# Rows of small blocks scattered from the tile of their sums instead of a copy

## The chip, the cores and the metric

The kernel runs on one core of a Trainium2 chip. A core has TensorE (PE in the profile; PEld is its weight loads), VectorE (DVE), ScalarE (ACT), GpSimd (POOL), SyncE (SP), and DMA engines that all of them can give work to. The metric is the device time of one execution in microseconds; the median of several runs is compared.

## The reference

Sigmoid attention over 8 batches, 12 heads, 448 tokens and head size 64 gives 3584 rows of 768. These go through a mixture of experts in which each token takes one expert of 8 (hidden size 1024), or none.

```
scores = scale * (q @ k.T) - log(S);  attn = sigmoid(scores);  x = attn @ v   # as rows, 3584 x 768
compute = (x @ w_skip) > 0                     # other rows are returned as they are
e = argmax(x @ w_gate);  gate = softmax(x @ w_gate)[e]
out = x;  out[compute] = x + gate * (relu(x @ w1[e]) @ w2[e])
```

## The kernel before

The first part of the span (to about 327 us) is the attention, step by step over pairs of heads, and the first two blocks of the mixture of experts. Each attention row is stored to the output in DRAM, and each token's gate and number are put into a list per expert.

The rest is one loop whose length is known only at run time: one pass is one block of tokens of one expert. A block takes one of four arms (`choose`, line 1515):

- FULL: 128 tokens, with the expert's weights split into a high and a low part (three matmuls for each product).
- SPLIT: the same for the last full block of an expert, which also splits the next expert's weights on ScalarE and VectorE between its own steps.
- HALF: up to 64 tokens, with the weights as loaded (`raw1`, `raw2`), two columns of PE's array at once.
- FEW: up to 32 tokens, four columns at once (`few`, line 1375).

The order of the instructions is written out by hand (`manual_schedule`); the framework adds the waits between engines, and between one pass and the next, from which tiles are read and written. Those waits compare a semaphore with a number that grows by a fixed amount per pass; all four arms raise each semaphore by the same amount. Engines go from one pass to the next without a common barrier: while PE begins the next block's first product (`gemm1`, line 516), ScalarE and VectorE finish the block before.

What a FEW block does, in the names that matter below: PE forms `ph` (line 1381), ScalarE the relu `hs` (1398), PE turns it (1407), ScalarE copies it to `ht` (1409), and PE forms `py` (1381 again, the same helper). In between PE turns the next block's rows `xn` (492) and `fetch` (1256) has GpSimd gather the rows of the block after the next into `xn` and its record into `rn`. The sums of a FEW block lie in `py` in four pieces of 32 rows by 384. ScalarE writes two of them, times the gate, into `yt` (1434) and VectorE adds the other two (1436). `put` (1279) then runs on GpSimd: it copies the row numbers to `rp[0]` (1281) and once more (1282); `seen` (1287) adds two elements that straddle the end of a half, which makes GpSimd wait for the engine that wrote it; and `scatter` (570) is an indirect DMA on GpSimd's queue that adds the rows to the output. `advance` (1302) moves the records on by one block on VectorE: lines 1306, 1308, and 1309, which writes `rid`, the source of `rp[0]`.

FULL, SPLIT and HALF blocks write their sums straight into `ys` (`weigh_sum`, 1316, VectorE) and scatter from there. A FEW block's sums go from `yt` to `ys` by two copies on GpSimd (1296), and from `ys` to the output.

In the FULL arm, the instructions after a FEW block are, on ScalarE, the relu at line 525, `hh` (535), `hi_x` (498) and `whole_x` (1093); on VectorE `hl` (536); on PE `gemm1`, the transpose of `hs` (530) after the ninth matmul of the second half, and `gemm2` (543). In the SPLIT arm VectorE first has `lo1` (1228), and later `lo2` (1234).

Of the kernel before, what the change touches and what calls it, by code (L numbers as in the profile page):

```python
# [15 lines left out]
ALU = mybir.AluOpType  # L16
# [7 lines left out]
def kernel(  # L24
# [14 lines left out]
    NT, DM = out.shape  # L39
# [12 lines left out]
    H2 = DM // 2  # L52
# [5 lines left out]
    SM = 32  # L58
# [510 lines left out]
    def scatter(idx, src, op=ALU.bypass):  # L569
        return nc.gpsimd.indirect_dma_start(  # L570
            out=out[:, :],
            out_offset=bass.IndirectOffsetOnAxis(ap=idx, axis=0),
            in_=src,
            in_offset=None,
            bounds_check=NT - 1,
            oob_is_err=False,
            compute_op=op,
        )
# [93 lines left out]
    for n, (b, hp) in enumerate(steps):  # L672
# [39 lines left out]
        for c in range(4):  # L712
            at = wk.tile([P, 2, S], F32, tag="A", name=f"at_{b}_{hp}_{c}", bufs=5)
# [140 lines left out]
    ys = rows_pool.tile([P, DM], F32, name="ys")  # L854
# [326 lines left out]
    rp = [mo.tile([P, 1], I32, name=f"rp{j}") for j in range(2)]  # L1181
# [7 lines left out]
    yt = mo.tile([P, DM], F32, name="yt")  # L1189
# [46 lines left out]
    dve, pool = nc.vector, nc.gpsimd  # L1236
# [42 lines left out]
    def put(n, last=None):  # L1279

        pool.tensor_tensor(rp[0], rid[:, 0:1], zero, op=ALU.add)
        pool.tensor_tensor(rs, rp[0], zero, op=ALU.add)
        if last is False:
            pool.drain()

        def seen(y, at):
            pool.tensor_tensor(
                jk[:n], y[:n, at - 1 : at + 1], y[:n, at - 1 : at + 1], op=ALU.add
            )

        if n == SM:

            for o in range(2):
                seen(yt, (o + 1) * H2 - 1)
                s = slice(o * H2, (o + 1) * H2)
                pool.tensor_copy(ys[:n, s], yt[:n, s])
        seen(ys, H2)
        out_rows = scatter(rp[0][:n], ys[:n], ALU.add)
        tc.declare_no_dep(out_rows.ins, group="got", across_iterations=True, reason="a token is in one block only")
        tc.add_to_no_dep_group("put", out_rows.ins)  # L1300

# [16 lines left out]
    def block(i, last):  # L1318
# [48 lines left out]
        for o in range(2):  # L1367
            weigh_sum(ys[:, o * H2 : (o + 1) * H2], py[:, o, :H2], recs[:, 0, 0:1])
        put(P, last)
        advance(1 if last else 2)  # L1370
        if last:
# [3 lines left out]
    def few(i):  # L1375
# [52 lines left out]
        for m in range(2):  # L1428
            for o in range(2):
# [3 lines left out]
                if not m:  # L1433
# [3 lines left out]
                    yt[:SM, s], p, recs[:SM, 0, 0:1], yt[:SM, s], op0=ALU.mult, op1=ALU.add  # L1437
                )
        put(SM)
        advance()  # L1440

    def half(i):
# [54 lines left out]
        for o in range(2):  # L1497
            s = slice(o * H2, (o + 1) * H2)
            weigh_sum(ys[:MD, s], py[o * MD : (o + 1) * MD, 0, :H2], recs[:MD, 0, 0:1])
        put(MD)  # L1500
        advance()

# [55 lines left out]
```

## Time and profile before

| | us |
|---|---|
| median of 3 runs (lowest to highest) | 532.26 (531.96 to 532.32) |
| the profiled execution | 531.85 |
| its span, first to last instruction | 529.9 |
| PE busy in the span | 509.5 (96%) |
| GpSimd busy in the span | 257.9 (49%) |
| the ten copies of line 1296, 0.494 to 0.497 each | from 417.5 to 522.5 |

The span is what the profiler sees; the execution's time has a little more around it. In the rows of the profile the first numbers of a timeline row are its start and duration in us, then come engine, line, operation, output and inputs with their shapes; in brackets stands how long the engine had been idle and what ended that. "issue" there is an engine that waited for nothing the profile shows. PE's matmuls are pipelined and their ends are modelled.

The trace holds five FEW blocks (ten writes of `yt` at line 1434), at about 407, 433, 459, 485 and 511 us. Before the first, second, third and fifth of them lies a FULL block, before the fourth a SPLIT block. After the fifth the loop ends.

### The profile page before, as it was taken

How to read it: one execution, taken by the hardware profiler on the slowest of the kernel's cores; microseconds unless marked ns; L12 is line 12 of the kernel's file. 1: busy time of each engine (PE TensorE's matmuls, PEld its weight loads, DVE VectorE, ACT ScalarE, POOL GpSimd, SP SyncE). 2: the span in 40 equal slices, each digit the busy share in tenths (PEclk: the TensorE clock that was granted, in tenths of full speed). 3: DMA queues.
4: the chain of work that ended last, by engine and by line, in shares of the span. 5: the costliest groups of instructions: out<-in, count | busy, mean ns of one | idle time of the engine just before them, and what ended most of it. 6: DMA issues, size and time to landing. Idle time of an engine off the chain costs nothing.

```text
span 529.9 us, 14858 instructions
## 1 busy us (share of the span) xinstructions
PE 509.5 (96%) x4793; PEld 343.9 (65%) x4794; DVE 295.4 (56%) x721; ACT 281.0 (53%) x485; POOL 257.9 (49%) x404
## 2 busy tenths in 40 slices
PE   8999999999999999999999999999999999999991
PEld 6775555545545555456555989948678787878770
DVE  4556757648668577576674952862132222259422
ACT  5776776766767767677665211942212313268221
POOL 4523652444546676766664331553224444445553
PEclk9999999999999999999999999999999999999997
DMA  8999787897889999999865033969393959596951
GB/s 212 212 250 196 148 184 159 166 181 173 187 184 230 230 192 230 197 205 222 178 122 109 11 91 106 397 205 345 92 377 113 344 207 348 206 341 217 326 170 31
DMA packets 140288, 107.21 MB, mean 202 GB/s; under 512 B 97099, under 2 KB 112731, under 8 KB 140240
## 3 DMA queue, kind: packets, MB, share of 16 engines
q1 hardware_dynamic: 134000, 97.66, 69.5%
q0 software_dynamic: 4576, 8.65, 7.2%
q8 instruction: 30, 0.49, 0.4%
q10 hardware_dynamic: 1664, 0.26, 0.3%
q14 instruction: 18, 0.15, 0.1%
HBM read 98.49 MB, written 17.56 MB: 219 GB/s over the span
## 4 chain that ended last, share of the span: by engine, by line
PE 82%; DVE 7%; DMA 3%; issue 2%; ACT 2%; SPq 2%; POOL 1%; POOLq 0%; ACTq 0%; DVEq 0%
PE s L212 19%; PE pa L240 18%; PE ph L516 11%; PE py L543 11%; PE b_ph L516 3%; PE b_py L543 3%; PE py L1381 3%; DVE x L194 2%; PE ph L1381 2%; PE py L1448 2%; PE ph L1448 2%; PE pxt L492 2%; DMA kq<-in_q_dram 1%; SPq L263 1%; PE pl L280 1%
## 5 line engine op out<-in xcount | busy, mean ns | idle before, releaser
L232 ACT ACTIVATE at<-s,bias 128x896 f32<-128x896 f32 (+1 forms) x191 | 173.5, 914 | 84.4 <-PE s L212 72.6
L212 PE MATMUL s<-x 64*64 64x448 f32 (+1 forms) x1528 | 171.8, 497 | 4.2 <-DVE pos L395 3.1
L240 PE MATMUL pa<-at,v 64*64 64x448 f32 (+1 forms) x1536 | 170.0, 489 | 0.0
L176 POOL COPY kq<-kq 32x896 f32<-32x896 f32 (+1 forms) x96 | 87.6, 913 | 87.9 <-DMA kq<-in_q_dram 50.2
L212 PEld LDWEIGHTS s<-x 64*64 64x64 f32 x1528 | 86.3, 191 | 51.6 <-issue 20.9
L240 PEld LDWEIGHTS pa<-at,v 64*64 64x64 f32 x1536 | 68.7, 133 | 52.0 <-issue 38.2
L194 DVE STREAM_TRANSPOSE x<-kq 128x448 f32<-128x448 f32 x94 | 81.9, 934 | 5.2 <-POOL kq L176 5.2
L250 DVE TENSOR_TENSOR xt<-xt,pa 128x448 f32<-128x448 f32 x48 | 29.7, 620 | 58.7 <-ACT xt L669 56.5
L486 POOL TENSOR_TENSOR wl<-wr,wh 128x384 fp32r<-128x384 f32 (+1 forms) x28 | 31.2, 1126 | 21.7 <-DVE wh L485 17.1
L414 POOL DMA_INDIRECT lst<-rec,idx x32 | 31.4, 980 | 17.5 <-issue 6.1
L255 DVE STREAM_TRANSPOSE y<-xt 128x448 f32<-128x448 f32 x48 | 31.0, 645 | 5.4 <-DMA out_dram<-y 4.0
L570 POOL DMA_INDIRECT out_dram<-ys,rp x15 | 23.7, 1579 | 16.4 <-issue 8.2
L543 PE MATMUL py<-wh,hh 128*128 128x384 f32 x112 | 29.8, 347 | 0.0
L525 ACT ACTIVATE hs<-ph 128x512 f32<-128x512 f32 x14 | 8.4, 597 | 39.8 <-PE ph L516 31.8
L536 DVE TENSOR_TENSOR hl<-pht,hh 128x512 fp32r<-128x512 f32 x14 | 9.7, 690 | 35.3 <-ACT hh L535 23.4
L543 PE MATMUL py<-wh,hl 128*128 128x384 f32 x112 | 28.9, 339 | 0.0
L543 PE MATMUL py<-wl,hh 128*128 128x384 f32 x112 | 28.7, 337 | 0.0
L502 DVE TENSOR_TENSOR xl<-pxt,xh 128x384 fp32r<-128x384 f32 x30 | 15.3, 551 | 20.4 <-PE py L1381 4.5
L516 PE MATMUL ph<-wl,xh 128*128 128x512 f32 x84 | 26.6, 403 | 0.0
L669 ACT ACTIVATE xt<-pa 128x448 f32<-128x448 f32 x48 | 25.8, 537 | 0.8 <-PE pa L240 0.8
L516 PE MATMUL ph<-wh,xh 128*128 128x512 f32 x84 | 25.7, 402 | 0.0
L1316 DVE TENSOR_SCALAR ys<-py,recs 128x384 f32<-128x384 f32 (+1 forms) x18 | 10.4, 611 | 25.8 <-PE py L543 20.7
(275 smaller groups left out, 690.4 us busy)
## 6 DMA issues: line engine op xcount, KB each, us to landing
raw<-in_moe_w_dram SPq DMA_DIRECT2D x64, 768.0 KB
v<-in_v_dram SPq DMA_DIRECT2D x48, 256.0 KB
out_dram<-y SPq DMA_DIRECT2D x192, 56.0 KB
kq<-in_k_dram SPq DMA_DIRECT2D x46, 224.0 KB
kq<-in_q_dram SPq DMA_DIRECT2D x46, 224.0 KB
wr<-in_moe_w_dram SPq DMA_DIRECT2D x12, 256.0 KB
wr<-in_moe_w_dram SPq DMA_DIRECT2D x16, 192.0 KB
lst<-fill SPq DMA_DIRECT2D x4, 464.0 KB
```

The lines of the kernel that those rows point to most:

```text
L176: nc.gpsimd.tensor_copy(a[BT:, :, :, :BT], a[:BT, :, :, BT:])
L194: nc.vector.transpose(xs[:, n].rearrange("p (r j) -> p j r", j=NJ), t.rearrange("p (j d) -> p j d", d=D)[:, :, :BT],)
L212: nc.tensor.matmul(sc[m * D : (m + 1) * D, j, : qs.stop - qs.start], xs[r, 0, first::NR7], xs[r, 1, qs], start=True, stop=True,)
L232: nc.scalar.activation(at[:, :, :n], sc[:, :, :n], AF.Sigmoid, bias=bias, scale=SCALE)
L240: nc.tensor.matmul(pa[j * D : (j + 1) * D, r, qs], vt[rs, j, r + c if c < 3 else 3 * (1 - r), :], at[rs, j, : qs.stop - qs.start], start=( ...
L250: nc.vector.tensor_tensor(x, x, pa[:, 1, :S], op=ALU.add)
L255: nc.vector.transpose(y, xts[b][:, hp, :])
L414: put = nc.gpsimd.indirect_dma_start(out=lst[:, :], out_offset=bass.IndirectOffsetOnAxis(ap=idx[:, c : c + 1], axis=0), in_=rec[:, c, :], ...
L486: nc.gpsimd.tensor_tensor(lo, r, hi, op=ALU.subtract)
L516: nc.tensor.matmul(ph[h], a[:, j * P : (j + 1) * P], w[j][h], start=(n == 0), stop=(n == len(t) - 1),)
L543: last = nc.tensor.matmul(py[:, o, :H2], a[h][:, js], w[j][:, o * H2 : (o + 1) * H2], start=(j == 0 and n == 0), stop=(j == NK2 - 1 and n ...
L1381: nc.tensor.matmul(dst[g * SM : (g + 1) * SM, :n], a, w, start=(j == 0), stop=(j == most - 1), tile_position=(0, g * SM),)
```

## The change

In `put`, a FEW block's rows are scattered from `yt` itself. The two copies to `ys` and the look at `ys` behind them go; the looks at the end of each half of `yt` stay. Blocks of the other arms do as before.

```
-        if n == SM:
-
-            for o in range(2):
-                seen(yt, (o + 1) * H2 - 1)
-                s = slice(o * H2, (o + 1) * H2)
-                pool.tensor_copy(ys[:n, s], yt[:n, s])
-        seen(ys, H2)
-        out_rows = scatter(rp[0][:n], ys[:n], ALU.add)
+        rows = yt if n == SM else ys
+        for at in ((H2 - 1, DM - 1) if n == SM else (H2,)):
+            seen(rows, at)
+        out_rows = scatter(rp[0][:n], rows[:n], ALU.add)
```

(`SM` is 32, `DM` 768, `H2` 384; `n` is the number of tokens of the arm.)

## The prediction

> **What bounds the kernel now.** I read the page first: TensorE (PE) is busy for 96% of the span. So an engine beside it, such as GpSimd (POOL), matters only where PE waits for it, or after PE's last matmul.
>
> ```profile
> span 529.9 us, 14858 instructions
> PE 509.5 (96%) x4793; PEld 343.9 (65%) x4794; DVE 295.4 (56%) x721; ACT 281.0 (53%) x485; POOL 257.9 (49%) x404
> ```
>
> Next I asked for the two tiles of the change. The copy that goes is a group of 10, two in each of five FEW blocks. Then came the waits from 400 us on, which is where those blocks lie.
>
> ```profile
> L1296 POOL COPY ys<-yt x10: 494/496/497, 417.5 to 522.5; 32x384 f32<-32x384 f32 x10
> POOL rp L1281 <- DMA out_dram<-ys,rp: 8.2, 4, 4.0
> POOL xn L1259 <- PE pxt L492: 7.4, 3, 2.5
> ACT hs L525 <- PE ph L516: 9.3, 4, 3.1
> ```
>
> The first number of a wait is its total in us, then its count and its longest. The second row is the one to keep: at line 1281 GpSimd overwrites rp[0], the indices that the scatter of the block before reads, and four times it had to wait for that scatter's DMA to finish. So "the scatter of the block before has finished" is an event that a FEW block can reach too early, by up to 4.0 us as GpSimd arrives there. The third says that after a scatter GpSimd mostly has nothing to do until PE has read xn (line 492): an earlier scatter in mid-kernel has no one behind it.
>
> The place where the copy does lie on the chain of waits is the end, since the last block is a FEW block. First its row in the chain, then rows of the timeline there (start, duration, engine), with two of the block before for comparison:
>
> ```profile
> 522.46 0.49 POOL ys L1296
> 512.17 0.19 POOL L1287 TENSOR_TENSOR jk<-ys 128x2 f32<-128x2 f32 x1 [3.21 <-DVE sv L1306]
> 512.94 1.62 POOL L570 DMA_INDIRECT out_dram<-ys,rp  x1 [0.58 <-issue]
> ...
> 518.89 0.20 POOL L1281 TENSOR_TENSOR rp<-rid,zero 128x1 int32<-128x1 int32 x1
> 519.72 1.17 ACT L1434 ACTIVATE yt<-py,recs 32x384 f32<-32x384 f32 x2 [2.44 <-PE py L1381]
> 521.56 0.62 DVE L1436 SCALAR_TENSOR_TENSOR yt<-py,recs,yt 32x384 f32<-32x384 f32 x1
> 522.33 0.19 POOL L1287 TENSOR_TENSOR jk<-yt 32x2 f32<-32x2 f32 x1
> 523.82 1.41 POOL L570 DMA_INDIRECT out_dram<-ys,rp  x1 [0.60 <-issue]
> ```
>
> **Part 1, removed: two copies and one look-up per FEW block, five times.** In the first four blocks I cost this at nothing: the cover is GpSimd's idle time before line 1259 (the wait row above, up to 2.5 us), and if it were gone the gain would still be only GpSimd's. In the last block the scatter ends the kernel, so the gain counts in full. VectorE's second half of yt ends at 521.56 + 0.62 = 522.18. The second look-up (line 1287) then starts somewhere between 522.18 and its present 522.33; it no longer has a copy ahead of it. From a look-up to the scatter behind it the block before took 512.94 - 512.17 = 0.77 us. So the scatter starts between 522.95 and 523.10 instead of 523.82: 0.72 to 0.87 us earlier, and I take **-0.8**. Nothing else ends later than this scatter, so the span shortens by the same amount. The scatter itself still moves 32 rows: no change of its duration.
>
> **Part 2, moved: who reads yt last.** Before, the last reader of yt was GpSimd's copy, done a few us after the block. Now it is the DMA. ScalarE's next write of yt (line 1434) must wait until that DMA has finished. yt is scattered only in FEW blocks, and the one before is far back (415.51, 467.90 and 492.41 below, with a block of another kind between any two). But the four arms are branches of one loop body, every pass issues exactly one scatter from line 570, and the waits between passes are counts per pass. I take it that the count to wait for is that of the pass before, whatever its arm: the same event that line 1281 waits for. Then line 1434, on ScalarE, cannot start before about the time at which line 1281 starts in the same block, wherever 1281 itself had to wait. The rows for the first, third and fourth FEW block (those of the fifth are above):
>
> ```profile
> 415.51 1.17 ACT L1434 ACTIVATE yt<-py,recs 32x384 f32<-32x384 f32 x2 [2.54 <-PE ph L516]
> 416.03 0.19 POOL L1281 TENSOR_TENSOR rp<-rid,zero 128x1 int32<-128x1 int32 x1 [1.41 <-DMA out_dram<-ys,rp]
> ...
> 467.90 1.18 ACT L1434 ACTIVATE yt<-py,recs 32x384 f32<-32x384 f32 x2 [2.56 <-PE ph L516]
> 468.81 0.18 POOL L1281 TENSOR_TENSOR rp<-rid,zero 128x1 int32<-128x1 int32 x1 [1.79 <-DMA out_dram<-ys,rp]
> 470.80 0.15 DVE L1309 CAST rid<-recs 128x1 int32<-128x1 f32 x1
> 471.13 0.60 ACT L525 ACTIVATE hs<-ph 128x512 f32<-128x512 f32 x1 [2.05 <-PE ph L516]
> ...
> 488.47 2.24 POOL L570 DMA_INDIRECT out_dram<-ys,rp  x1 [0.57 <-issue]
> 492.41 1.18 ACT L1434 ACTIVATE yt<-py,recs 32x384 f32<-32x384 f32 x2 [1.48 <-POOL rx L1263]
> 496.70 0.60 ACT L525 ACTIVATE hs<-ph 128x512 f32<-128x512 f32 x1 [3.12 <-PE ph L516]
> 498.52 0.60 PE L530 MATMUL pht<-ident,hs 128*128 128x128 f32 x4
> 499.92 0.18 POOL L1281 TENSOR_TENSOR rp<-rid,zero 128x1 int32<-128x1 int32 x1 [4.03 <-DMA out_dram<-ys,rp]
> 500.19 0.15 DVE L1309 CAST rid<-recs 128x1 int32<-128x1 f32 x1 [4.90 <-POOL rp L1281]
> 501.67 0.69 DVE L536 TENSOR_TENSOR hl<-pht,hh 128x512 fp32r<-128x512 f32 x1 [1.32 <-issue]
> 502.41 0.30 PEld L543 LDWEIGHTS py<-wh,hl 128*128 128x128 f32 x2 [0.16 <-DVE hl L536]
> ```
>
> ScalarE would be held by 0.5, 0.9 and **7.5** us, and by 0 in the fifth block, where 518.89 lies before 519.72. In the second GpSimd waits 8.2 - 1.41 - 1.79 - 4.03 = 1.0 us, less than in the first, a block of the same kind after one of the same kind: so 0.1 there. What is queued behind it on ScalarE is the relu of the next block (line 525), and behind that PE's transpose of hs (line 530). That relu waits for PE anyway, four times and 9.3 us in all: 2.05 us after the third FEW block, more than the 0.9, 3.12 after the fourth, and so 4.1 after the first two together, against 0.5 and 0.1. I cost these three at nothing; if that idle time were gone, they would add up to 1.5.
>
> The fourth FEW block follows the SPLIT block, whose scatter, issued at 488.47, finished only at 499.92. There the cover is too thin. ScalarE needs the time from its first write of yt to being ready at line 525 in the next pass:
>
> ```profile
> L525 ACTq EVENT_SEMAPHORE  x3: 17/38/38, 493.6 to 501.3; - x3
> 514.43 0.29 ACT hs L1398
> 514.72 0.14 issue
> ```
>
> 493.6 - 492.41 = 1.2 us (second write, branch, loading the next kind). So: release 499.92, relu starts at 501.1, ends 0.60 later at 501.7, and PE starts 0.14 after a relu (in the chain, between line 1398's and the transpose of it), at 501.85. Now it starts at 498.52. PE stands still for **3.3 us**, and everything after it is PE-bound up to the end.
>
> VectorE is late as well, but less than PE: line 1309 came 470.80 - 467.90 = 2.9 us after ScalarE's write in the third block, so here at 502.8; hl (line 536) starts 501.67 - 500.19 = 1.5 after that, at 504.3, and is done at 505.0. PE asks for it 502.25 - 498.52 = 3.7 us after its transpose, now at 505.6. So there is no second stall, and the 0.16 us that PE waits for hl today come back.
>
> **Can the release itself move?** The 0.9 us of the third block delay VectorE's end of that block. The SPLIT block that follows keeps VectorE packed:
>
> ```profile
> 469.11 1.26 DVE L1436 SCALAR_TENSOR_TENSOR yt<-py,recs,yt 32x384 f32<-32x384 f32 x2 [2.57 <-ACT yt L1434]
> 472.95 1.90 DVE L1228 TENSOR_TENSOR wl<-raw,wh 128x512 fp32r<-128x512 f32 x3 [2.00 <-PE ph L516]
> 466.60:485.10 18.50, 18.50 (x103) 16.48 (x103) 13.76 (x28) 14.78 (x28) 10.52 (x20) 1.00 0.92 332
> ```
>
> In the last row (a stretch's length, then busy time and count of PE, its weight loads, VectorE, ScalarE, GpSimd, clock, DMA share and GB/s) VectorE has 13.76 busy of 18.5. Of the idle 4.74, 2.57 and 2.00 lie before 473. If the 2.00 are the branch into the next pass, a late start is handed on and the SPLIT block's sums, with its scatter (488.47), come 0.9 us later; if they are a wait for PE, as the label has it, nothing moves. PE's own matmuls have slack for either. If the scatter's end follows in full, the stall is 3.3 + 0.9 = 4.2 us; if not at all, 3.3. I take the middle, **3.75**. The Trainium skill bears on this, "DMA: Bandwidth & Descriptors", section "SWDGE vs HWDGE vs iDMA": each DMA engine goes round-robin over its queues, GpSimd's among them. By that rule the scatter shares with the loads from when it is issued, which speaks for the upper end, a sum of +3.3; no row of this trace separates the two ends.
>
> **Sum.** +3.75 (PE waits) - 0.16 (hl) - 0.8 (end) = **+2.8 us**, between 3.3 - 0.16 - 0.87 = +2.3 and 4.2 - 0.16 - 0.72 = +3.3. The profiled execution took 531.85 us (span 529.9 and 1.95 around it), so it would take 534.65. It lies 0.4 below the median of the runs, 532.26; against the median the sum gives **535.1**.
>
> **Rivals.** (a) *The wait is for the last FEW block's scatter only*, because the bookkeeping knows that no other arm reads yt. Then nothing is added and the end's gain stands alone: 532.26 - 0.8 = 531.5, 0.15% down. For it: only one arm has the tile. Against: one loop body, one line that scatters, and the rows of line 1281, where a FEW block waits for the SPLIT block's scatter. It decides where line 1434 is released before 498.52 - 1.2 - 0.60 - 0.14 = 496.6, when no stall is left; break-even with the 0.96 gained is at a release of 497.5, 2.4 us before the one in the trace. This is the rival on the other side: not slower.
>
> (b) *The clock falls in the stall.* The trace has one long idle stretch of PE, the end:
>
> ```profile
> 523.00:524.00 1.00, 0.00 (x0) 0.00 (x0) 0.00 (x0) 0.00 (x0) 0.36 (x2) 0.84 0.00 0
> 524.00:525.00 1.00, 0.00 (x0) 0.00 (x0) 0.00 (x0) 0.00 (x0) 1.00 (x1) 0.50 0.00 0
> L1553 PEldq DRAIN  x3: 8/13/3092, 516.5 to 529.4; - x3
> ```
>
> PE had drained at 516.5 + 3.09 = 519.6; a mean clock of 0.84 in 523 to 524 puts the fall to 0.50 at 523.7, so 4.1 us later. A stall of 3.3 to 4.2 us lies just short of that. Where it did fall, no row shows how long it takes to come back: from nothing to the rest of that block at half speed (498.5 to 510.9, +12). Taking the same 4.1 us for the way back, at half speed, 2 us are lost: 535.1 + 2.0 = 537.1. The Trainium skill says, "TensorE: Matmul & The Clock Gate", "Part 1: The HAM clock gate", that one whole free-running window of about 3.4 us without work halves the clock and a like window of work restores it; by that figure the loss is about 1.7 us, and a stall of 3.75 us would only now and then contain a whole window. The trace's 4.1 us agrees, with a window that began some 0.7 us after the last matmul.
>
> (c) *The end does not gain*, because something other than the scatter releases the last steps: 535.1 + 0.8 = 535.9. In 523 to 525 the two rows have no DMA traffic and no engine but GpSimd at work, which speaks against it.
>
> **Chances.** A measurement of this kernel can tell about 0.2% (1.06 us) from no change. The forecast, a stall of 3 to 5 us with the end's gain: 0.75. (a) 0.11. (b) 0.07. (c) 0.04. The remaining 0.03 is for a stall that is partly absorbed, or a gain I do not see. All but (a) and half the rest are slower: slower 0.87, same 0.11, faster 0.02. For the forecast alone the range is 534.2 (2.3 on the profiled execution's time) to 535.6 (3.3 on the median). The 8-in-10 range takes in (c) and most of (b) and leaves out (a): 533.7 to 537.0.
>
> **What would show it.** In the trace after: no line 1296; in the fourth FEW block line 1434 at 499.9 to 500.9 instead of 492.4, its idle time ended by the DMA of out_dram, the first relu of the next block at 501 to 502, and a wait of PE at line 530 of 3 to 4 us "until ACT hs"; the first three FEW blocks without a wait of PE; from the last look-up to the scatter 0.8 and the scatter 0.8 us nearer to VectorE's last write. I am wrong if line 1434 of the fourth block still starts with PE's end (rival a), if the SPLIT block's scatter finishes several us sooner, or if the granted clock of that stage is below 1.00 (rival b).

## The result, and the profile after

| | before | after |
|---|---|---|
| median, us (lowest to highest) | 532.11 (531.94 to 532.32) | 535.46 (534.31 to 535.64) |
| the profiled execution, us (span) | 531.85 (529.9) | 535.44 (533.5) |

The medians differ by 3.35 us. The ratio on record is that of the fast runs, 1.0074 (interval 1.0054 to 1.0095), and need not equal the quotient of the two medians, here 1.0063; so with the ratios below. The prediction was 535.1, in a range of 533.7 to 537.0. In code behind line 1296 the new line numbers are four lower: ScalarE's write of yt is line 1430, VectorE's 1432, the record's copy to rid 1305.

First the head of the page after, which is as good as unchanged: PE is still busy for 96% of a longer span.

```profile
span 533.5 us, 14838 instructions
PE 510.6 (96%) x4793; PEld 344.9 (65%) x4794; DVE 296.3 (56%) x721; ACT 280.6 (53%) x485; POOL 251.7 (47%) x389
```

Then the waits from 400 us on (total in us, count, longest):

```profile
ACT yt L1430 <- DMA out_dram<-ys,rp: 17.7, 4, 8.4
POOL rp L1281 <- DMA out_dram<-ys,rp: 7.4, 4, 3.1
PE pht L530 <- ACT hs L525: 2.7, 1, 2.7
```

The first row is new: ScalarE's write of yt waits for a scatter from **ys**, a tile it never touches. It is the scatter of the pass before, whichever arm issued it. The third row is new too, and is the price: PE waits for a relu once. The timeline of the fourth FEW block shows it link by link:

```profile
490.18 2.24 POOL L570 DMA_INDIRECT out_dram<-ys,rp  x1 [0.57 <-issue]
500.74 0.18 POOL L1281 TENSOR_TENSOR rp<-rid,zero 128x1 int32<-128x1 int32 x1 [3.15 <-DMA out_dram<-ys,rp]
500.77 1.17 ACT L1430 ACTIVATE yt<-py,recs 32x384 f32<-32x384 f32 x2 [8.42 <-DMA out_dram<-ys,rp]
502.13 0.60 ACT L525 ACTIVATE hs<-ph 128x512 f32<-128x512 f32 x1 [0.19 <-ACT yt L1430]
502.87 0.63 PE L530 MATMUL pht<-ident,hs 128*128 128x128 f32 x4 [2.71 <-ACT hs L525]
505.12 0.69 DVE L536 TENSOR_TENSOR hl<-pht,hh 128x512 fp32r<-128x512 f32 x1 [1.32 <-ACT hh L535]
```

The SPLIT block's scatter goes out at 490.18. Its end, 10.6 us later, releases lines 1281 and 1430 within 0.03 us of each other; then come the two writes, the relu and PE's transpose. At the end of the span:

```profile
525.16 1.26 DVE L1432 SCALAR_TENSOR_TENSOR yt<-py,recs,yt 32x384 f32<-32x384 f32 x2 [2.46 <-ACT yt L1430]
526.57 0.18 POOL L1287 TENSOR_TENSOR jk<-yt 32x2 f32<-32x2 f32 x1 [0.53 <-DVE sv L1302]
527.36 1.39 POOL L570 DMA_INDIRECT out_dram<-yt,rp  x1 [0.61 <-issue]
```

From VectorE's last write to the scatter it is now 527.36 - 526.42 = 0.94 us; before, 523.82 - 522.18 = 1.64.

Part of the difference stands far ahead of the change. SyncE's loads before the loop, and ScalarE's first instruction behind them, first in the timeline of before, then of after:

```profile
328.95 3.08 SPq L1216 DMA_DIRECT2D raw<-in_moe_w_dram  x4
332.30 1.68 ACT L1225 ACTIVATE wh<-raw 128x512 fp32r<-128x512 f32 x3 [0.71 <-SPq L1527]
```

```profile
329.49 4.38 SPq L1216 DMA_DIRECT2D raw<-in_moe_w_dram  x4
334.14 1.68 ACT L1225 ACTIVATE wh<-raw 128x512 fp32r<-128x512 f32 x3 [2.20 <-SPq L1523]
```

Four loads took 1.3 us longer to issue, in code that the change does not touch, and the scatter of the first SPLIT block went out at 350.26 instead of 348.42. The balance of the two profiled executions, in us:

- The scatter ahead of the first FEW block is 1.39 late (410.09 against 408.69).
- PE's matmuls right ahead of the transpose in the fourth block are 1.49 late (499.31 against 497.82), so 0.10 more.
- Had PE gone on, its transpose would have started at 498.52 + 1.49 = 500.01. It starts at 502.87, which is 2.86 of stall; the row's own wait of 2.71 is a little less, since the ends of PE's work are modelled.
- ScalarE's first write in the fifth block is 4.24 late (523.96 against 519.72), so 0.11 came back on the way, the wait for hl among it.
- The end gains 1.64 - 0.94 = 0.70.

That makes 1.39 + 0.10 + 2.86 - 0.11 - 0.70 = 3.54, by which the last scatter starts later (527.36 against 523.82); the spans differ by 3.6. Without the 1.39 the change itself costs 2.15 us in this execution, where 2.8 were predicted.

### The profile page after: what moved, and what is told of

It is laid out like the page before. It is cut to its first block, busy times and chain, and to the rows that moved or that the text cites. A ratio compares the mean times of both kernels' runs of the same rounds, so it can differ in the third digit from the quotient of the medians.

```text
span 533.5 us, 14838 instructions
## 1 busy us (share of the span) xinstructions
PE 510.6 (96%) x4793; PEld 344.9 (65%) x4794; DVE 296.3 (56%) x721; ACT 280.6 (53%) x485; POOL 251.7 (47%) x389
## 4 chain that ended last, share of the span: by engine, by line
PE 78%; DMA 6%; DVE 6%; ACT 3%; issue 2%; SPq 2%; POOL 1%; ACTq 0%; POOLq 0%; DVEq 0%
PE s L212 19%; PE pa L240 18%; PE py L543 11%; PE ph L516 10%; PE b_ph L516 3%; PE b_py L543 3%; DMA kq<-in_q_dram 2%; PE ph L1377 2%; PE py L1444 2%; PE ph L1444 2%; DMA out_dram<-ys,rp 2%; PE py L1377 2%; PE pxt L492 2%; DVE x L194 2%; SPq L263 1%
## 5 line engine op out<-in xcount | busy, mean ns | idle before, releaser
L240 PEld LDWEIGHTS pa<-at,v 64*64 64x64 f32 x1536 | 70.7, 133 | 51.5 <-issue 38.7
L516 PE MATMUL ph<-wh,xl 128*128 128x512 f32 x84 | 24.5, 395 | 0.0
```

The costliest lines, as they stand in the source:

```text
L240: nc.tensor.matmul(pa[j * D : (j + 1) * D, r, qs], vt[rs, j, r + c if c < 3 else 3 * (1 - r), :], at[rs, j, : qs.stop - qs.start], start=( ...
L516: nc.tensor.matmul(ph[h], a[:, j * P : (j + 1) * P], w[j][h], start=(n == 0), stop=(n == len(t) - 1),)
```

## The experiments

All ran on other chips than the profile above, where the kernel before has medians of 527.30 (first four), 527.11 (next four) and 527.16 (last two). A ratio is to the kernel before on the same chip. Theory A throughout: the end of the scatter of the pass before releases ScalarE's write of yt, and that is what the change costs.

**The changed kernel once more.** No edit.

> The changed kernel once more. Theory A: what costs is ScalarE's wait at its first write of yt in the fourth FEW block (PE stands 2.7 us or more), less 0.7 to 0.8 at the end; the 1.4 us by which the first profile was already late at the first FEW block are chance (SyncE's loads ahead of the loop were slow to be taken). Then the median is 534.3 to 535.5, and in this profile the first write of yt comes near 415.5 to 416.1 if the first pass is not late again. Rival B: the change makes the first SPLIT pass late every time: the first FEW block is 1.4 us late again, and the stall explains only half of the loss.

Measured: 529.45 us, ratio 1.0048 (1.0024 to 1.0073). Its timeline, first and fourth FEW block:

```profile
418.60 1.17 ACT L1430 ACTIVATE yt<-py,recs 32x384 f32<-32x384 f32 x2 [6.73 <-DMA out_dram<-ys,rp]
420.68 0.63 PE L530 MATMUL pht<-ident,hs 128*128 128x128 f32 x4 [1.01 <-ACT hs L525]
496.58 1.17 ACT L1430 ACTIVATE yt<-py,recs 32x384 f32<-32x384 f32 x2 [6.79 <-DMA out_dram<-ys,rp]
498.69 0.63 PE L530 MATMUL pht<-ident,hs 128*128 128x128 f32 x4 [1.15 <-ACT hs L525]
```

The early lateness is not there (the scatter of the first SPLIT block goes out 20.55 us after the scatter ahead of it, at 327.52; in the profile before it was 20.45, from 327.97 to 348.42, and in the profile after 21.95), so the change does not bring it every time. The six later profiles without added work have 20.46 to 20.67 there; why the profile after has 21.95 stays open. But PE now stops twice for about 1 us: the first FEW block, which I had called free, stops it when its scatter takes 10.3 us instead of 7.0.

**The wait without the gain.** The copies and the look at ys stay, but the scatter reads yt.

```
+        if n == SM:
+            for o in range(2):
+                seen(yt, (o + 1) * H2 - 1)
+                pool.tensor_copy(ys[:n, s], yt[:n, s])
+        seen(ys, H2)
+        out_rows = scatter(rp[0][:n], (yt if n == SM else ys)[:n], ALU.add)
```

> The two copies and the look at ys stay as before, but the scatter reads yt: part 2 (the wait) without part 1. Theory A: the wait without the end's gain, 0.7 to 0.8 slower than the changed kernel: 535.0 to 536.3, with PE waiting at line 530 in the pass after the fourth FEW block. If the loss came from the shorter list of GpSimd's instructions (rival B), this kernel, which has the old list, is at 532.3 plus 2.7 at most.

Measured: 529.37 us, ratio 1.0042 (1.0014 to 1.0069). Its runs spread from 526.86 to 538.00. The wait alone costs as much as the whole change, within the intervals; the 0.8 us by which it was to be worse could not be resolved.

**The gain without the wait.** The copies go, and the scatter reads ys, which FEW blocks then do not fill: their sums are left out of the output.

```
-        out_rows = scatter(rp[0][:n], rows[:n], ALU.add)
+        out_rows = scatter(rp[0][:n], ys[:n], ALU.add)
```

> The copies and the look at ys are gone, and the scatter reads ys, which no one has filled: the sums of the FEW blocks are left out. Part 1 without part 2: yt is read by GpSimd's looks only. Theory A: no wait of ScalarE for a DMA, the end 0.7 to 0.8 earlier: 531.3 to 531.6. Rival B: 1.4 more, 532.7 to 533.0.

Measured: 526.55 us, ratio 0.9990 (0.9970 to 1.0011). Its waits:

```profile
ACT yt L1430 <- PE py L1377: 7.5, 5, 1.5
POOL rp L1281 <- DMA out_dram<-ys,rp: 5.3, 2, 3.5
```

GpSimd still waits for scatters, ScalarE for PE only, and PE nowhere for the relu. Against the changed kernel on the same chip, the wait costs 529.45 - 526.55 = 2.9 us; each of the two intervals is over 1 us wide to either side.

**The wait on another engine.** VectorE's addition, the last step of the sum, writes into ys; the scatter reads ys; there is no copy.

```
-                    yt[:SM, s], p, recs[:SM, 0, 0:1], yt[:SM, s], op0=ALU.mult, op1=ALU.add
+                    ys[:SM, s], p, recs[:SM, 0, 0:1], yt[:SM, s], op0=ALU.mult, op1=ALU.add
```

> ScalarE writes its two pieces to yt as before, VectorE adds the others and writes the sums to ys, and the scatter reads ys: no copies, and the wait for the scatter of the pass before lies on VectorE. Theory A: in the fourth FEW block VectorE is released at about 500.0 to 500.7, its two sums and the records take 1.7, and hl starts 1.5 after line 1305, at 503.2 to 503.9, done at 503.9 to 504.6, where PE asks for it at 502.25: a stall of 1.6 to 2.3 on another line of PE (543), less 0.8 at the end: 533.1 to 533.8. If only ScalarE's place in the order mattered and VectorE had room, 531.4.

Measured: 526.79 us, ratio 0.9989 (0.9972 to 1.0006). The wait is on VectorE as expected. The stall of PE of 1.6 to 2.3 us did not come, so that part was a miss: it was worked out from a scatter of 11.45 us, and here the scatter took 9.5 us (485.52 to 495.04). The fourth FEW block:

```profile
495.09 1.26 DVE L1432 SCALAR_TENSOR_TENSOR ys<-py,recs,yt 32x384 f32<-32x384 f32 x2 [4.83 <-PE ph L516]
498.24 0.69 DVE L536 TENSOR_TENSOR hl<-pht,hh 128x512 fp32r<-128x512 f32 x1 [1.32 <-issue]
499.73 0.51 PE L543 MATMUL py<-wh,hl 128*128 128x384 f32 x2
```

The addition starts 0.05 us after line 1281, which the scatter's end releases at 495.04; so "PE" in its bracket is not what came last. hl is done at 498.93 and PE asks for it at 499.73: 0.8 us to spare. VectorE's next result is needed by PE only after its transpose, the relu before it. As this was the best version so far, it ran again:

> The kernel with VectorE's last addition written into ys and scattered from there, once more, since 0.9989 (0.9972 to 1.0006) did not tell it from before. Theory: no copy on GpSimd, so the end gains 0.7 to 0.8 us; the wait for the scatter of the pass before is on VectorE's addition and not on ScalarE, and hl behind it has the slack of line 1281's path, less the 0.4 us or so by which the addition is longer. Ratio 0.9985, with no wait of PE at line 530; where the scatter takes over 11 us, a wait of PE at line 543 of 1 to 2 us and a ratio of 1.001. Rival (any wait for that scatter costs what it costs on ScalarE): 1.003 to 1.006.

Measured: 526.14 us, ratio 0.9982 (0.9968 to 0.9996), no wait of PE for hs or hl. Against the kernel before, only this second run sets the version apart, by 1.0 us and narrowly. It clearly beats the changed kernel, by 2.7 us (526.79 against 529.45, where both ran on one chip).

**What makes the scatter long.** In a FEW block the loads of the next expert's weights bring 8 rows each.

```
-            raw1g[h, g],
-            w1[ds(nx[0], 1), g * 3 * P : (g + 1) * 3 * P, h * H1 : (h + 1) * H1]...
+            raw1g[h, g][0:8, 0, :],
+            w1[ds(nx[0], 1), g * 3 * P : g * 3 * P + 8, h * H1 : (h + 1) * H1]...
```

> The changed kernel, in which a FEW block's eight loads of the next expert's weights bring 8 rows of each tile instead of all; the later blocks then multiply with the first expert's weights, so that only the traffic is left out. Theory A (the scatter of the pass before takes 8 to 11 us because those loads run beside it): the one scatter of 128 rows with no loads beside it, in the last two blocks of the kernel before, ended within 518.89 - 512.94 = 5.95 us. So in the fourth FEW block it ends about 6 us after its issue instead of 9.2 to 11.5; ScalarE's first write of yt, which could start 4 us after that issue, is held by 2 us, the relu behind it had 3.1 us to spare, and PE has no wait at line 530 for hs. The time is that of before less the 0.8 us of the end: ratio 0.998 to 1.000. Rival (the scatter is slow by itself, 128 rows that are read, added to and written): 9 to 11 us from issue to release as before, a wait of PE of 1 to 3 us, ratio 1.002 to 1.006.

Measured: 527.02 us, ratio 0.9997 (0.9982 to 1.0012). The fourth FEW block (lines are 14 higher than in the changed kernel):

```profile
485.95 2.25 POOL L570 DMA_INDIRECT out_dram<-ys,rp  x1 [0.57 <-issue]
492.56 1.17 ACT L1444 ACTIVATE yt<-py,recs 32x384 f32<-32x384 f32 x2 [4.04 <-DMA out_dram<-ys,rp]
494.30 0.60 ACT L525 ACTIVATE hs<-ph 128x512 f32<-128x512 f32 x1 [0.57 <-PE ph L516]
```

The scatter is over after 6.6 us, against 9.2 to 11.5 with full loads beside it. ScalarE is still held, but the relu waits for PE by 0.57 us and not the other way round. So the loads make the scatter late enough to hurt.

**A later scatter.** GpSimd first adds ys to itself into a spare tile ahead of a SPLIT block's scatter; here in the changed kernel, then in the kernel before.

```
+        if last:
+            pool.tensor_tensor(spare, ys, ys, op=ALU.add)
         out_rows = scatter(rp[0][:n], rows[:n], ALU.add)
```

> The changed kernel, in which GpSimd first adds ys to itself into a spare tile before a SPLIT block's scatter (128 x 768; line 486 took 1.28 us for 128 x 512, so about 1.9 us). Theory A (the scatter's end sets ScalarE's write in the fourth FEW block): everything behind it comes 1.9 us later, PE's wait at line 530 grows from the 1.1 to 2.7 seen to 3.0 to 4.6 us, and the time by 1.9 us: ratio to before 1.007 to 1.010 on a chip where the changed kernel has 1.0048. Rival (b) of the prediction rides on it: if PE idles for more than about 4 us, the granted clock falls below 1.00 behind the wait and 2 us or more come on top: ratio 1.011 or above. Rival (the scatter's end is set by the loads beside it and not by its start): no change, ratio 1.003 to 1.006.

Measured: 530.86 us, ratio 1.0078 (1.0052 to 1.0104). The changed kernel had 1.0048 (1.0024 to 1.0073) on another chip; the intervals overlap, so the medians alone do not show the 1.9 us that were expected. The profile shows the step itself. The addition took 1.46 us and put the scatter 1.0 us later: it starts 1.78 us after the look ahead of it (486.37), where the repeat of the changed kernel has 0.77. The scatter took 9.6 us (9.2 in the repeat), and PE waited 2.26 us at line 530 (1.15 in the repeat). That is more than in the repeat, as theory A has it, but less than the 3.0 to 4.6 us expected.

```profile
486.52 1.46 POOL L1296 TENSOR_TENSOR spare<-ys 128x768 f32<-128x768 f32 x1
488.15 2.14 POOL L570 DMA_INDIRECT out_dram<-ys,rp  x1 [0.16 <-issue]
497.71 1.17 ACT L1433 ACTIVATE yt<-py,recs 32x384 f32<-32x384 f32 x2 [7.90 <-DMA out_dram<-ys,rp]
499.82 0.63 PE L530 MATMUL pht<-ident,hs 128*128 128x128 f32 x4 [2.26 <-ACT hs L525]
```

In the stretches around it (length, then PE's busy time; the third number from the right is the granted clock) rival (b) of the prediction appears:

```profile
498.00:499.00 1.00, 0.00 (x0) 0.00 (x0) 0.08 (x1) 0.86 (x2) 0.13 (x1) 1.00 1.05 395
500.50:501.00 0.50, 0.50 (x4) 0.40 (x3) 0.21 (x2) 0.50 (x1) 0.00 (x1) 0.99 1.05 395
503.00:504.00 1.00, 1.00 (x5) 0.73 (x4) 0.00 (x0) 0.18 (x1) 0.00 (x0) 0.50 1.03 402
504.00:504.50 0.50, 0.50 (x5) 0.50 (x4) 0.00 (x0) 0.42 (x1) 0.44 (x4) 0.59 1.06 412
```

PE is at work again when the clock falls, at 500.99; it is back at 504.41 (0.59 is 0.82 of that half at 0.50). For 3.42 us PE runs at half speed.

> The same addition of about 1.9 us ahead of a SPLIT block's scatter, in the kernel before. There ScalarE waits for nothing, and the path is line 1281 of GpSimd, then rid and hl on VectorE, then PE at line 543. In the profile of before, where the scatter took 11.45 us, PE waited 0.16 us for hl, so that path had no slack and 1.9 us more would cost 1.9; with a scatter of 9.3 us it has 2.0 us of slack, and costs nothing. So: ratio 1.000 where the scatter takes about 9.3 us, up to 1.0035 where it takes 11.5, and the wait of PE stands at line 543 for hl, never at line 530. Rival (before is insensitive to this scatter altogether): 1.000 with no wait of PE for hl even where the release comes later than 500.0 less the shift of the execution.

Measured: 526.94 us, ratio 0.9992 (0.9974 to 1.0010). The scatter took 9.9 us, and the path over VectorE had slack, as expected for that length:

```profile
495.88 0.18 POOL L1282 TENSOR_TENSOR rp<-rid,zero 128x1 int32<-128x1 int32 x1 [2.52 <-DMA out_dram<-ys,rp]
497.61 0.69 DVE L536 TENSOR_TENSOR hl<-pht,hh 128x512 fp32r<-128x512 f32 x1 [1.31 <-issue]
499.19 0.51 PE L543 MATMUL py<-wh,hl 128*128 128x384 f32 x2
```

hl is there at 498.30, 0.9 us ahead of PE. With the same addition, and on the same chip, the changed kernel has 1.0078 and the kernel before nothing that can be measured.

**How short a stall lowers the clock.** The same with two and with three additions (each line added to `put` moves the later line numbers by one).

> As the kernel with one addition of 128 x 768 on GpSimd (1.46 us) ahead of a SPLIT block's scatter, with two. Theory A: PE's wait at line 530 behind the fourth FEW block grows from 2.26 to about 3.7 us and the time by another 1.4 us, to 532.3 where the kernel before has 527.1 (ratio 1.010). On top comes what the clock does. In the profile with one addition PE stood from 497.56 to 499.82, and the granted clock was 0.50 from 501.0 to 504.4, which is 1.7 us lost; in the profile of the changed kernel PE stood from 500.17 to 502.87 and it stayed at 1.00. Clock theory C (fixed stretches of 3.4 us, and one in which PE is idle for 2.3 us or more halves the next): a gap of 3.7 us has such a stretch in 74 of 100 positions, so most runs are at about 534.0 (ratio 1.013) with some at 532.3. Clock theory W (only a whole idle stretch of 3.4 us counts): 0.3 / 3.4, 9 in 100 runs at 534.0, the median at 532.3.

> The same with three additions of 1.46 us. Theory A: PE waits about 5.2 us at line 530 behind the fourth FEW block, and the time without the clock is 533.8 where before has 527.1 (ratio 1.0127). Clock theory C: a gap of 5.2 us holds 2.3 us of some stretch of 3.4 us in every position, so all runs lose 1.7 us or more: 535.5 (ratio 1.016), and the profile has a stretch of 0.50. Clock theory W: 1.8 / 3.4, about half of the runs at 535.5 and half at 533.8.

Measured: 534.12 us, ratio 1.0145 (1.0112 to 1.0178), and 537.01, ratio 1.0202 (1.0178 to 1.0226). The medians do not separate the two clock theories, since the additions cost more than planned: they took 3.60 and 5.74 us, and they slowed VectorE, whose four subtractions took 3.56 us in the kernel before:

```profile
488.26 3.56 DVE L1234 TENSOR_TENSOR wl<-raw,wh 128x768 fp32r<-128x768 f32 x4
```

With three additions beside them, and PE waiting behind them for VectorE:

```profile
483.12 7.02 DVE L1235 TENSOR_TENSOR wl<-raw,wh 128x768 fp32r<-128x768 f32 x4
490.29 1.67 PE L516 MATMUL ph<-wl,xh 128*128 128x512 f32 x6 [1.36 <-DVE recs L1313]
```

The profiles do separate them. With three additions, PE stands from 495.46 (a first stretch with 0.46 of work) to 500.72:

```profile
495.00:496.00 1.00, 0.46 (x2) 0.01 (x1) 0.00 (x0) 0.00 (x0) 0.07 (x1) 1.00 1.10 264
497.00:498.00 1.00, 0.00 (x0) 0.00 (x0) 0.00 (x0) 0.00 (x0) 0.00 (x0) 0.80 0.97 326
501.00:504.00 3.00, 3.00 (x10) 2.51 (x9) 1.38 (x8) 0.60 (x1) 1.59 (x2) 0.50 0.54 209
504.00:505.00 1.00, 1.00 (x5) 0.72 (x5) 0.00 (x0) 0.00 (x0) 0.00 (x0) 0.79 0.73 89
```

The clock falls at 497.60 (0.80 is 0.4 of that stretch at 0.50), only 2.14 us after PE stopped, and returns at 504.42, so 6.82 us later, twice 3.41. If the grid is one of 3.41 us, the stretch before the fall held 2.14 us of idle time; with one addition it held 2.23 (497.59 to 499.82). Theory W, a whole idle stretch, falls; theory C fits, with a limit at or below 2.14 us where it had taken 2.3.

The ends of the spans settle the grid, because the clock falls there too, after PE's last matmul. With one addition the two falls, at 500.99 and 524.89, lie seven times 3.41 us apart; with two, 506.67 and 530.56, seven times; with three, 497.60 and 524.90, eight times. Counted back from the fall at the end in steps of 3.41 us, all twelve profiles say the same: every stretch with 2.07 us or more without work of PE is followed by one at 0.50, and every stretch with 1.80 us or less by one at 1.00. So the limit lies between the two, by PE's ends as the profile models them. At the end of the profile after, the drain of PE comes 1.1 us behind that modelled end; the stalls inside the kernel, which do not depend on it, have 1.80 without a fall and 2.14 with one. The profile after, in four of its stretches:

```profile
501.07:504.48 3.41, 1.61 (x9) 1.44 (x10) 1.76 (x7) 2.04 (x4) 0.80 (x4) 1.00 1.04 403
504.48:507.89 3.41, 3.41 (x23) 3.12 (x22) 0.77 (x2) 0.60 (x1) 2.33 (x9) 1.00 1.04 404
521.55:524.96 3.41, 1.20 (x16) 0.42 (x8) 1.05 (x4) 0.98 (x2) 1.66 (x4) 1.00 0.28 58
524.96:528.37 3.41, 0.00 (x0) 0.00 (x0) 1.75 (x7) 0.17 (x1) 1.38 (x3) 0.50 0.00 0
```

An edge of the grid at 501.07 cut its stall of 2.71 us into 0.90 and 1.80, so the clock stayed; at the end 2.21 us fell into one stretch.

The mean granted clock of each execution says how often it fell. A stretch at half speed takes 0.003 off the mean of a span; the part behind PE's end, 5.4 to 8.5 us in the profiles, leaves at least 0.992. The kernel before (78 executions beside the experiments) and the versions with lighter loads or without ScalarE's wait (12 each) never go below 0.992. The changed kernel has 0.990 in one of its first four executions and 0.990 or 0.991 in three of the twelve of its repeat; with the copies kept it is 0.988 and 0.991 in two of twelve; with one addition it is 0.988 to 0.991 in six of nine, with two and three in all. So the fall of the clock is a part of what the wait costs, in some executions.

The runs with additions also make theory A firmer. With none (the repeat), one, two and three additions the SPLIT block's scatter starts 0.85, 1.86, 3.99 and 6.13 us after the last sum, and takes 9.2, 9.6, 9.4 and 10.0 us: its end follows its start.

The profiled execution with two additions, 539.19 us, has one more thing to show, in its waits:

```profile
PE pht L530 <- ACT hs L525: 6.2, 4, 3.8
PE py L543 <- DVE hl L536: 1.3, 1, 1.3
```

Its scatters before the first three FEW blocks, which the edit does not touch, took 10.3, 10.1 and 9.5 us, and each of the three stopped PE (1.01, 0.84, 0.55). Behind the third VectorE was late as well.

## Why the prediction was right, and where it was not

**The mechanism held.** The wait is for the pass before and not for the last FEW block (rival a is out), it sits on ScalarE's first write of yt, and it stops PE at line 530 in the fourth FEW block, behind the SPLIT block. The run with the wait on VectorE, the runs with lighter loads and with a later scatter, and the run without the wait all moved the way this says, the later scatter by less than expected.

**The stall was mis-sized: 3.75 us predicted, 2.86 measured.** The step that failed is "Can the release itself move?", with the release that it starts from. Two of its terms were too large:

- The scatter was taken at 11.45 us, the one length at hand. It took 10.59 us in the profile after, 0.86 less, and 9.2 to 10.0 in every later profile with full loads. The length varies from execution to execution.
- The third block's delay was taken at 0.9 us. Its scatter took 7.1 us, and ScalarE's first write came at 469.62 instead of 467.90, 0.33 later than the 1.39 by which all was late.

Whether that delay is handed on, which the prediction left open and split in the middle, is settled by the rows of the profile after:

```profile
472.51 0.16 DVE L1305 CAST rid<-recs 128x1 int32<-128x1 f32 x1
474.66 1.90 DVE L1228 TENSOR_TENSOR wl<-raw,wh 128x512 fp32r<-128x512 f32 x3 [2.00 <-PE pht L530]
```

VectorE comes to the SPLIT block 2.0 us behind its last instruction of the FEW block, as before, and 474.66 - 472.95 = 1.71 us late, while PE is 1.4 late there. So the 2.00 were not a wait for PE, the small delay was handed on whole, and the scatter too came 1.71 late. Against PE, which was 1.49 late by then, that is 0.22. The way from the release to the transpose took 2.10 us, 0.17 more than the 1.93 of the prediction. With these terms its sum is 3.33 - 0.86 + 0.22 + 0.17 = 2.86, the measured stall: its arithmetic was right.

Across runs, PE's wait in the fourth block was the release, counted from the scatter's issue, less 7.9 to 8.3 us (10.59 and 2.71; 9.21 and 1.15; with the copies kept 9.40 and 1.08).

The rule of the Trainium skill that stood beside this, the round-robin over queues in "DMA: Bandwidth & Descriptors", section "SWDGE vs HWDGE vs iDMA", speaks of shared engines; the runs agree that the loads stretch the scatter (6.6 us with light ones), and that a later scatter ends later. How it shares with them packet by packet no run shows.

**"These three cost nothing" was true of one execution only.** In the profile after, scatters of 7.0 to 7.9 us ahead of the first three FEW blocks stopped nothing. At 9.0 us (the first block with the copies kept) PE did not wait either, at 9.5 it waited 0.55, at 9.9 0.57, at 10.3 1.0. So the cover is about 9.0 to 9.3 us of scatter, and I had taken it from the one execution where the scatters were short.

**The end gained 0.70, against 0.8.** The terms of look-up and copy were right to 0.1 us, and rival (c) is out. Its share in the medians is seen only in the versions without the wait: 0.9990 and 0.9982, the second clear of 1.

**What the sum did not have** is the 1.4 us ahead of the loop, in code that the change does not touch. In the profiled execution they are there; whether the other three had them is not known. Without them the change's own 2.15 us would have made 532.11 + 2.15 = 534.3 and not 535.46; the repeat on another chip also rose by 2.15 us, though with two stalls of about 1 us instead of one. So it is partly luck that 535.46 lies so near to 535.1: the stall was 0.9 too large, and a term of 1.4 was missing.

**Rival (b)**, the clock, was not in the profile after, but that too was luck: the stall lay across an edge of the grid, and in another of the four executions the mean clock of 0.990 says that it fell. The prediction's reason to give it little was that a stall of 3.3 to 4.2 us lies just short of the 4.1 us from PE's drain to the fall. The same distance is only 1.1 us at the end of the profile after, where PE has drained at 520.8 + 3.07 = 523.87 and the clock falls at 524.96:

```profile
L1549 PEldq DRAIN  x3: 8/13/3068, 520.8 to 533.0; - x3
```

So the reason was wrong: the distance depends on where PE stops on the grid. The price given for (b), 1.7 to 2.0 us, was about right: 3.42 us at half speed.

## What to carry to other kernels

In a loop of several arms whose waits are counts per pass, as here, a tile that a DMA reads is not free for its next writer until the DMA of the pass before has ended, even if another arm issued it on another tile. Put that wait on the engine whose next result is needed last, here VectorE's addition instead of ScalarE's multiplication, and the same saving had no cost that could be measured. Take the length of a scatter from several executions, not one: beside heavy loads it is a range, and slack that covers its short end does not cover its long one.

## What the runs showed of the hardware

- A scatter of 128 rows took 5.7 to 6.6 us from issue to release with light loads beside it, and 5.6 to 11.5 with full ones. It varied at the same place of the same kernel (ahead of the first FEW block: 7.0 and 10.3).
- A PE stall of 2.2 us inside a busy kernel can halve the granted clock for 3.4 us, after work has begun again. What counts is the idle time in one stretch of a fixed grid of 3.41 us: by PE's modelled ends, 2.07 us or more halved the next stretch, 1.80 or less did not, in all twelve profiles. The Trainium skill, "TensorE: Matmul & The Clock Gate", "Part 1: The HAM clock gate", asks for a whole idle window of about 3.4 us; the length of the grid agrees with the 3.41 and 3.42 us seen, the need for a whole idle one does not, since windows with 2.14 and 2.23 us of idle time were enough.
- GpSimd's additions of 128 x 768 held up VectorE's subtractions on other tiles: 3.56 us became 4.48 with one, 5.75 with two, 7.02 with three. From the first start to the last end the two engines took 4.9, 6.2 and 7.4 us, nearly the sum of their times alone (3.56 and 1.46 for each addition: 5.0, 6.5, 7.9). The Trainium skill, "SBUF — State Buffer", section "SBUF: two separate sides", has the rule, an exclusive lock on a port shared by the two engines for an operation of VectorE with two inputs in SBUF against one of GpSimd that reads it; these numbers agree.
